# One value unit loaded in two parts: 80 partitions by the GpSimd queue, 48 by the SyncE queue

## The chip, the cores and the metric

The kernel runs on one core of a Trainium2 chip. The metric is the device time of one execution in microseconds (us), as the median of several runs. Kernels that are compared ran on the same chip in alternation. The spans in the profile are shorter than the times by about 2 us.

Words used below: a *DMA engine* is one of the sixteen that move bytes for this core. *SP* is SyncE, whose queue issues nearly all loads; *POOL* is GpSimd. A *share* is one partition's row of 16 KB; it moves as one packet (the trace of the kernel before has 9216 packets of 16,384 bytes for its 72 loads of 128 such rows). A *completion* is one of the sixteen increments of a load's semaphore that DMA makes (the traces record sixteen for each of these loads); that each of the sixteen engines makes one when its part has landed is how the author reads them.

## The reference, cut to what matters

One token goes through two branches, whose results are mixed by a gate. The heavy branch is attention over a long cache.

```
q = (x @ wq)                              # 32 heads of 128; x is [1, 1, 1024]
k_cache, v_cache: [1, 4, 65536, 128] bf16 # 64 MB each: read once
scores = q k^T * 128**-0.5; p = softmax(scores); o = p v
a = o @ wo
b = mixer(x, w_in, w_sp, b_sp, w_out)     # 7 + 4 MB of weights
out = g * a + (1 - g) * b                 # g = sigmoid(sum(x * gate_w))
```

All in all 162 MB come from HBM for very little arithmetic.

## The kernel before

The caches are read in units of 8192 keys, 2 MB each. A unit is `[128 partitions, 8192]` in bf16: partition p holds 64 keys that follow one another, so a partition's row is 16 KB in one piece. Loads go into a ring of nine slots, in one order, all from the SP queue. A slot is loaded again as soon as TensorE has read it.

```python
def kv(cache, g, u):
    return cache[0, g, UK * u:UK * (u + 1), :].rearrange("(p x) d -> p (x d)", p=128)
...
def issue(upto):
    while issued[0] < min(upto, len(stream)):
        n = issued[0]
        assert n < NS or stream[n - NS][0] in used
        key, src, ln = stream[n]
        s = n % NS
        P("SP", lambda e, n=n, src=src, ln=ln: e.dma_start(slot(n)[:, 0:ln], src), w=[("slot", s)], dma="s%d" % s)
        issued[0] += 1
...
# the order: wq (4 loads); then K units, with w_in and w_out between them;
# from the ninth K unit on a K and a V unit in turn; then V units; then wo (4 loads)
...
def pv_piece(n):                      # one V unit: 16 matmuls
    sl, key = use(("v", n))
    ...
    P("PE", f, r=[("ptsb", n % 2), key], w=[B(OB)])
    issue(place[("v", n)] + NS + 1)
```

Of the kernel before, what the change touches and what calls it, by code (L numbers as in the profile page):

```python
# [8 lines left out]
ALU = mybir.AluOpType  # L9
# [7 lines left out]
class Recorder:  # L17
# [7 lines left out]
        self.readers = {}  # L25
        self.dma_count = {}

    def op(self, eng, fn, r=(), w=(), dma=None):
        o = Op()
        o.eng, o.fn, o.inc, o.count = eng, fn, False, 0  # L30
        o.dma = None
        deps = {}
        for k in r:
            if k in self.writer:
                deps[id(self.writer[k])] = (self.writer[k], True)
        for k in w:
            if k in self.writer:
                deps.setdefault(id(self.writer[k]), (self.writer[k], False))
            for x in self.readers.get(k, ()):
                deps.setdefault(id(x), (x, False))  # L40
        o.deps = list(deps.values())
        for k in r:
            self.readers.setdefault(k, []).append(o)
        for k in w:
            self.writer[k] = o
            self.readers[k] = []
        if dma is not None:
            self.dma_count[dma] = self.dma_count.get(dma, 0) + 16
            o.dma = (dma, self.dma_count[dma])
        o.idx = len(self.ops)  # L50
        self.ops.append(o)
        return o
# [85 lines left out]
def bass_gated_mix__gqa_block_cached__mixer_gmlp__decode_kernel(  # L138
# [23 lines left out]
    FC = FH // 128  # L162
# [3 lines left out]
    NU = Sk // UK  # L166
# [5 lines left out]
    QW = DO // 4  # L172
# [9 lines left out]
    def region(name, nbf):  # L182
        nonlocal cur
        OFF[name] = cur
        cur += (nbf + 31) // 32 * 32

    for name, n in [
        ("RING", NS * SLOT), ("KT", NKTS * 1024), ("SC", NSC * 1024), ("PSB", 1024), ("PTSB", 1024),
        ("QPAD", G * 128), ("IDB", 128), ("IDF", 256), ("BM", 256), ("ONES", 256), ("SEL", 16 * 32),
        ("M16", 32), ("M8", 16), ("M32", 64), ("MQ", 32), ("OT", 256), ("XT", KC), ("GW", KC), ("WB", 2), ("MAXC", 2 * G * NU), ("LP", 2 * G * NU),  # L190
        ("COLS", 2 * 64), ("DM", 32), ("OSB", 1024), ("OSC", 512), ("OV", OC), ("Z", 2 * 28), ("Z2", 2 * 28),
        ("ZG", 2 * 28), ("ZE", 2 * 28), ("YB", FC), ("BROW", 2 * QW), ("OROW", QW),
    ]:
        region(name, n)
    NA = (cur + 63) // 64 * 64
# [2 lines left out]
    def ab(name, n, o=0):  # L198
        return arena[:, OFF[name] + o:OFF[name] + o + n]
# [4 lines left out]
    def vw(base, off, dims, p0=0, np_=128):  # L204
        ps = base.ap[0][0]
        return bass.AP(tensor=base.tensor, offset=base.offset + off + p0 * ps,
                       ap=[[ps, np_]] + [list(d) for d in dims])
# [19 lines left out]
    def slot(n):  # L227
        return ab("RING", SLOT, (n % NS) * SLOT)
# [4 lines left out]
    ptsb = lambda i: ab("PTSB", 512, 512 * (i % 2))  # L233
# [3 lines left out]
    SCB, PTB, OB, MB = 4, 5, 6, 7  # L237
# [4 lines left out]
    P = R.op  # L242

    def B(i):
        return ("bank", i)
# [35 lines left out]
    WQ_N = HQ * Dh  # L281
# [20 lines left out]
    for n in range(NU, total + NU + 1):  # L302
        k = n if n < total else None
        v = n - NU - 1
# [4 lines left out]
        else:  # L309
            v = None  # L310
# [3 lines left out]

    issued = [0]

    def issue(upto):
        while issued[0] < min(upto, len(stream)):
            n = issued[0]
            assert n < NS or stream[n - NS][0] in used  # L320
            key, src, ln = stream[n]
            s = n % NS
            P("SP", lambda e, n=n, src=src, ln=ln: e.dma_start(slot(n)[:, 0:ln], src), w=[("slot", s)], dma="s%d" % s)
            issued[0] += 1

    used = set()
# [1 line left out]
    def use(key):  # L328
        issue(place[key] + 1)
        used.add(key)  # L330
        return slot(place[key]), ("slot", place[key] % NS)

    issue(NS)


    P("DVE", lambda e: e.tensor_reduce(m8, vw(idf, 0, [[1, 8], [8, 16]]), AXX, ALU.add), r=["idf"], w=["m8"])
# [5 lines left out]
      r=["m32"], w=["sel"])  # L342
# [6 lines left out]
      r=["ones", "gs"], w=[B(PTB)])  # L349
# [4 lines left out]
      r=["g"], w=["omg"])  # L354


    for i in range(4):
        sl, key = use(("wq", i))

        def f(e, i=i, sl=sl):  # L360
            for k in range(2):
                for h in range(HQ):
                    ins = e.matmul(pf(OB)[:, h:h + 1], sl[:, WQ_N * k + 128 * h:WQ_N * k + 128 * (h + 1)],  # L363
                                   xT[:, 2 * i + k:2 * i + k + 1], start=(i == 0 and k == 0 and h == 0),
                                   stop=(i == 3 and k == 1), skip_group_check=True)
            return ins
        P("PE", f, r=["xT", key], w=[B(OB)])
        issue(place[("wq", i)] + NS + 1)
    for g in range(G):
        P("DVE", lambda e, g=g: e.tensor_copy(vw(qpad, 128 * g, [[40, 4], [1, 8]]),  # L370
                                              vw(pf(OB), 8 * g, [[0, 4], [1, 8]])),
          r=[B(OB)], w=["qpad"])
# [75 lines left out]
    def pv_piece(n):  # L448
        g, u = KV[n]
        sl, key = use(("v", n))  # L450

        def f(e):
            for xi in range(4):
                for cg in range(4):
                    ins = e.matmul(pf(OB)[32 * cg:32 * (cg + 1), :],  # L455
                                   ptsb(n)[:, 128 * xi + 32 * cg:128 * xi + 32 * (cg + 1)],
                                   vw(sl, 128 * (4 * cg + xi), [[2048, 4], [1, 128]]),
                                   start=(u == 0 and xi == 0), stop=(u == NU - 1 and xi == 3),
                                   tile_position=(0, 32 * cg), skip_group_check=True)
            return ins  # L460
        P("PE", f, r=[("ptsb", n % 2), key], w=[B(OB)])
        issue(place[("v", n)] + NS + 1)
        if u == NU - 1:
            out_piece(g)
# [104 lines left out]
    for si, (k, v, aux) in enumerate(steps):  # L569
        nxt = steps[si + 1][1] if si + 1 < len(steps) else None  # L570
        if k is None and pend:
            s_piece()
        if v is not None and v not in started:
            start_exp(v)
        for j in range(4):
            if k is not None:
                k_piece(k, j)
                s_piece() if len(pend) > 1 else None
            if j == 1 and v is not None:
                pt_piece(v)  # L580
            if j == 2 and nxt is not None and (k is not None or not pend):
                start_exp(nxt)
            if j == 3 and v is not None:
                pv_piece(v)
        if v is not None and v % NU == 0:
            weight_piece(v // NU)
        if aux is not None:
            (win_piece if aux[0] == "win" else wout_piece)(aux[1])
# [3 lines left out]
    for i in range(4):  # L592
        sl, key = use(("wo", i))
# [11 lines left out]
      r=["brow"], w=["orow", B(FB)])  # L605
# [32 lines left out]
```

## Time and profile before

| | before |
|---|---|
| time, median of the first three runs | 395.02 us (394.99 to 395.49) |
| span in the profile | 393.2 us |
| DMA, slices 3 to 38 | 419 to 430 GB/s |
| TensorE busy | 70% |
| the last load's sixteen completions | 381.95 to 388.62 us |

These are lines of the profile page of the kernel before: the span; the busy tenths and the rate of DMA in 40 equal slices; the DMA queues with packets, megabytes and their share of sixteen engines' span (q1 is the SP queue, q8 carries instructions); the chain of waits by engine and by line; and issues of loads, with the median time from issue to landing.

```profile
span 393.2 us, 8544 instructions
DMA  8999999999999999999999999999999999999992
GB/s 318 403 427 422 419 429 423 423 423 428 430 427 427 424 425 425 427 427 426 423 423 425 427 428 428 427 428 428 427 425 427 421 428 425 427 426 430 425 397 89
q1 hardware_dynamic: 11240, 162.01, 97.3%
q8 instruction: 31, 0.51, 0.5%
DMA 60%; PE 31%; DVE 6%; ACT 1%; issue 1%; ACTq 0%; DVEq 0%
...
arena<-in_A_v_cache_dram SPq DMA_DIRECT2D x32, 2048.0 KB, 37.5
```

The rate is flat from the third slice to the end. Nothing but more rate, or fewer bytes, or a shorter tail can make this kernel faster. The next lines are the end of the chain of waits, in order of time (start, duration, what):

```profile
346.71 41.91 DMA arena<-in_A_wo_dram
388.62 0.14 issue
388.76 1.91 PE pb L598 x26
390.69 0.42 DVE arena L604
```

The last completion of the last load, at 388.62 us, releases the last 1.9 us of matmuls. What counts is therefore the slowest DMA engine's last completion. The semaphore records in the trace give the sixteen completions of a load. Three of them, sorted (us):

```
landing near  40: 39.59 39.65 39.68 39.69 39.78 39.79 39.80 39.82 39.84 39.87 39.88 39.90 39.91 39.92 40.01 40.21
landing near 245: 240.07 240.15 240.19 240.21 240.22 240.64 240.77 242.13 243.34 243.39 243.44 244.89 244.93 244.97 244.99 245.18
the last load:    381.95 382.07 382.08 382.10 382.56 382.72 382.85 385.01 386.78 386.87 388.27 388.33 388.34 388.38 388.40 388.62
```

The engines drift apart, from 0.6 to 6.7 us. The drift grows in steps of about 1.4 us, one engine at a time, and each step falls on one of q8's 16 KB instruction packets (while 30 of these ran, between 46 and 373 us, the sixteen completions' lateness against the median of their first four, summed, grew from 2.9 to 52.1 us). At the end eight engines are late, and the other eight have nothing to do for up to 6.7 us. This is what the change aims at.

### The profile page before, as it was taken

The numbers are of one execution on the slowest core, as the hardware profiler recorded it, in microseconds if no ns is written. First come the engines' busy times: TensorE is split into PE (matmuls) and PEld (weight loads), VectorE is DVE, ScalarE is ACT, GpSimd is POOL, SyncE is SP. The second block draws the span as 40 slices with busy tenths as digits, with TensorE's granted clock in tenths as the row PEclk, the third lists the DMA queues.
The fourth block names the chain that finished last, engine by engine and source line by source line (L and its number), as shares of the span: only waits on it lengthen the run. The fifth ranks groups of instructions, "written<-read, shape, count | busy, mean of one in ns | idle before, by whom it ended". The sixth has DMA issues, their size and how long they took to land.

```text
span 393.2 us, 8544 instructions
## 1 busy us (share of the span) xinstructions
PE 275.8 (70%) x3902; PEld 195.3 (50%) x3902; DVE 160.4 (41%) x347; ACT 124.3 (32%) x171; POOL 1.5 (0%) x8
## 2 busy tenths in 40 slices
PE   0000699996998999997867686779668875644543
PEld 0000688885776766665645464556445553211121
DVE  2000043446666766576534354466334454200200
ACT  1000033332556555553524242335233334210000
POOL 1000000000000000000000000000000000000000
PEclk9999999886999999998989698889888898555555
DMA  8999999999999999999999999999999999999992
GB/s 318 403 427 422 419 429 423 423 423 428 430 427 427 424 425 425 427 427 426 423 423 425 427 428 428 427 428 428 427 425 427 421 428 425 427 426 430 425 397 89
DMA packets 12620, 162.57 MB, mean 413 GB/s; under 512 B 2596, under 2 KB 2600, under 8 KB 2600
## 3 DMA queue, kind: packets, MB, share of 16 engines
q1 hardware_dynamic: 11240, 162.01, 97.3%
q8 instruction: 31, 0.51, 0.5%
q10 hardware_dynamic: 1344, 0.00, 0.2%
q14 instruction: 5, 0.04, 0.0%
HBM read 162.01 MB, written 0.00 MB: 412 GB/s over the span
## 4 chain that ended last, share of the span: by engine, by line
DMA 60%; PE 31%; DVE 6%; ACT 1%; issue 1%; ACTq 0%; DVEq 0%
DMA arena<-in_A_k_cache_dram 30%; PE pb L388 16%; DMA arena<-in_A_wo_dram 11%; DMA arena<-in_gate_w_dram 10%; DMA arena<-in_A_v_cache_dram 10%; PE pb L410 6%; DVE arena L396 3%; PE pb L503 3%; PE pb L455 2%; PE pb L363 2%; DVE arena L415 2%; PE pb L443 1%; ACT arena L393 0%; PE pb L598 0%; PE pb L551 0%
## 5 line engine op out<-in xcount | busy, mean ns | idle before, releaser
L388 PE MATMUL pb<-arena 128*128 128x128 bf16 x2048 | 154.4, 236 | 27.5 <-DMA arena<-in_A_k_cache_dram 27.5
L388 PEld LDWEIGHTS pb<-arena 128*128 128x128 bf16 x2048 | 133.1, 107 | 55.6 <-DMA arena<-in_A_k_cache_dram 33.1
L396 DVE COPY arena<-pb 128x1024 bf16<-128x1024 bf16 x160 | 108.4, 689 | 109.8 <-PE pb L388 109.0
L393 ACT ACTIVATE arena<-pb 128x1024 bf16<-128x1024 bf16 x96 | 97.9, 1020 | 161.8 <-PE pb L388 161.8
L410 PE MATMUL pb<-arena 128*32 128x512 bf16 x512 | 54.9, 419 | 5.5 <-DVE arena L415 3.6
L455 PE MATMUL pb<-arena 128*32 128x512 bf16 x512 | 40.1, 441 | 19.0 <-DMA arena<-in_A_v_cache_dram 18.3
L455 PEld LDWEIGHTS pb<-arena 128*32 128x32 bf16 x512 | 14.3, 104 | 32.8 <-issue 20.2
L348 PE MATMUL pb<-arena 128*128 128x1 f32 x2 | 0.6, 362 | 40.7 <-DVE arena L347 40.7
L436 ACT ACTIVATE arena<-arena 128x512 bf16<-128x512 f32 x32 | 22.8, 713 | 16.3 <-PE pb L443 14.5
L446 DVE COPY arena<-pb 128x512 bf16<-128x512 bf16 x32 | 13.6, 424 | 30.4 <-PE pb L443 30.4
L410 PEld LDWEIGHTS pb<-arena 128*32 128x32 bf16 x512 | 13.3, 93 | 22.0 <-DVE arena L415 6.6
L415 DVE TENSOR_SCALAR_CACHE_REDUCE arena<-pb 128x512 f32<-128x512 f32 x32 | 21.8, 681 | 2.8 <-PE pb L410 2.8
L348 PEld LDWEIGHTS pb<-arena 128*128 128x128 f32 x2 | 0.5, 310 | 40.7 <-DVE arena L347 40.7
L443 PE MATMUL pb<-arena 128*128 128x128 bf16 x128 | 15.4, 257 | 0.0
L346 DVE TENSOR_TENSOR arena<-arena 128x8 f32<-128x8 bf16 x1 | 0.2, 166 | 37.0 <-DMA arena<-in_gate_w_dram 37.0
L443 PEld LDWEIGHTS pb<-arena 128*128 128x128 bf16 x128 | 9.1, 113 | 11.7 <-issue 11.7
L598 PE MATMUL pb<-arena 128*1 128x256 bf16 x128 | 7.5, 413 | 8.8 <-DMA arena<-in_A_wo_dram 8.8
L503 PEld LDWEIGHTS pb<-arena 128*128 128x128 bf16 x224 | 12.3, 153 | 0.9 <-issue 0.9
L503 PE MATMUL pb<-arena 128*128 128x1 bf16 x224 | 12.6, 192 | 0.0
L350 ACT ACTIVATE arena<-pb 128x1 f32<-128x1 f32 x1 | 0.2, 171 | 34.2 <-PE pb L348 34.2
L598 PEld LDWEIGHTS pb<-arena 128*1 128x1 bf16 x128 | 3.7, 115 | 12.3 <-DMA arena<-in_A_wo_dram 6.7
L363 PE MATMUL pb<-arena 128*128 128x1 bf16 x256 | 7.1, 165 | 1.8 <-issue 1.8
(78 smaller groups left out, 60.5 us busy)
## 6 DMA issues: line engine op xcount, KB each, us to landing
arena<-in_A_k_cache_dram SPq DMA_DIRECT2D x32, 2048.0 KB, 29.9
arena<-in_A_v_cache_dram SPq DMA_DIRECT2D x32, 2048.0 KB, 37.5
arena<-in_A_wq_dram SPq DMA_DIRECT2D x4, 2048.0 KB, 14.8
arena<-in_A_wo_dram SPq DMA_DIRECT2D x4, 2048.0 KB, 41.9
arena<-in_B_w_in_dram SPq DMA_DIRECT2D x4, 1792.0 KB, 22.5
arena<-in_B_w_out_dram SPq DMA_DIRECT2D x2, 1792.0 KB, 15.1
arena<-in_A_x_dram ACTq DMA_DIRECT2D x1, 2.0 KB, 22.3
arena<-in_gate_w_dram ACTq DMA_DIRECT2D x1, 2.0 KB, 39.0
```

The costliest lines, as they stand in the source:

```text
L363: ins = e.matmul(pf(OB)[:, h:h + 1], sl[:, WQ_N * k + 128 * h:WQ_N * k + 128 * (h + 1)], xT[:, 2 * i + k:2 * i + k + 1], start=(i == 0 and ...
L388: ins = e.transpose(pbf(pb)[:, 128 * t:128 * (t + 1)], sl[:, 128 * (8 * b + t):128 * (8 * b + t + 1)], idb)
L393: P("ACT", lambda e, i=i, pb=pb: e.activation(ktb(i), pbf(pb), ACTF.Copy), w=[("kt", i % NKTS), B(pb)])
L396: P("DVE", lambda e, i=i, pb=pb: e.tensor_copy(ktb(i), pbf(pb)), w=[("kt", i % NKTS), B(pb)])
L410: ins = e.matmul(pf(SCB)[32 * cg:32 * (cg + 1), :], qpad[:, 128 * g + 32 * j:128 * g + 32 * (j + 1)], src, start=(j == 0), stop=(j == 3), ...
L415: P("DVE", lambda e: e.tensor_scalar(scs(n), pf(SCB), 0.0, None, op0=ALU.add, op1=ALU.max, accum_out=maxc[:, n:n + 1]), w=[("sc", n % NSC) ...
L436: P("ACT", lambda e: e.activation(psb(n), scs(n), ACTF.Exp, bias=gcol(g, K_NB), scale=SCALE, accum_out=lp[:, n:n + 1]), r=[("sc", n % NSC) ...
L443: ins = e.transpose(pbf(PTB)[:, 128 * xi:128 * (xi + 1)], psb(n)[:, 128 * xi:128 * (xi + 1)], idb)
L446: P("DVE", lambda e: e.tensor_copy(ptsb(n), pbf(PTB)[:, 0:512]), w=[("ptsb", n % 2), B(PTB)])
L455: ins = e.matmul(pf(OB)[32 * cg:32 * (cg + 1), :], ptsb(n)[:, 128 * xi + 32 * cg:128 * xi + 32 * (cg + 1)], vw(sl, 128 * (4 * cg + xi), [[ ...
L503: ins = e.matmul(pf(MB)[:, z:z + 1], vw(sl, c0, [[7, 128]]), xT[:, 2 * i + k:2 * i + k + 1], start=(i == 0 and k == 0 and z == 0), stop=(i ...
L598: ins = e.matmul(pf(FB)[32 * q:32 * q + 1, 0:QW], ovec[:, 8 * i + c:8 * i + c + 1], sl[:, DO * c + QW * q:DO * c + QW * (q + 1)], start=(i ...
```

## The change

The intent is to give the early engines more of one unit and the late engines less. In the unit of group 2 with u = 0 (unit 16 of 32), partitions 0 to 79 come from the POOL queue in a copy whose source has an outermost dimension of 8, meant to have eight DMA engines carry ten shares each. Partitions 80 to 127 stay with SP, by the author's reckoning on sixteen engines with three shares each. Eight engines would then move 13 shares of this unit and eight move 3, where each moved 8. A tiny copy of 8 x 64 bytes ahead of it, on the same queue, is there to turn the queue's choice of engines. The rest of the diff (a scratch tile, an unused argument) is cut.

```diff
+    BAL = {("v", 2 * NU)}
+    HALF = 80
+    def eights(e, d, s_):
+        n = d.ap[-1][1]
+        m = d.ap[0][1] // 8
+        a = bass.AP(tensor=s_.tensor, offset=s_.offset, ap=[[m * n, 8], [n, m], [1, n]])
+        b = bass.AP(tensor=d.tensor, offset=d.offset, ap=[list(d.ap[0]), [1, 1], [1, n]])
+        return e.add_instruction(mybir.InstDMACopy(..., queue="qPoolDynamic", ins=e.lower_ap_dma(a), outs=e.lower_ap_dma(b)))
     def issue(upto):
 ...
-            P("SP", lambda e, n=n, src=src, ln=ln: e.dma_start(slot(n)[:, 0:ln], src), w=[("slot", s)], dma="s%d" % s)
+            p0 = HALF if key in BAL else 0
+            o = P("SP", lambda e, n=n, src=src, ln=ln, p0=p0: e.dma_start(slot(n)[p0:128, 0:ln], src[p0:128, :]),
+                  w=[("slot", s)], dma="s%d" % s)
+            if p0:
+                o2 = P("POOL", lambda e, n=n, src=src: eights(e, slot(n)[0:HALF, :], src[0:HALF, :]), w=["half"],
+                       dma="half")
+                o2.deps = list(o.deps)
 ...
     issue(NS)
+    P("POOL", ... InstDMACopy(..., ins: A_wq as [[WQ_N, 8], [1, 32]], outs: junk[0:8, :]) ..., dma="junk")
 ...
-        P("PE", f, r=[("ptsb", n % 2), key], w=[B(OB)])
+        P("PE", f, r=[("ptsb", n % 2), key] + (["half"] if ("v", n) in BAL else []), w=[B(OB)])
```

More of the change, by code (lines that the diff above doesn't have):

```diff
@@ L26, in __init__, with op @@
         self.dma_count = {}
-    def op(self, eng, fn, r=(), w=(), dma=None):
+    def op(self, eng, fn, r=(), w=(), dma=None, parts=1):
         o = Op()
@@ L47, in op @@
         if dma is not None:
-            self.dma_count[dma] = self.dma_count.get(dma, 0) + 16
+            self.dma_count[dma] = self.dma_count.get(dma, 0) + 16 * parts
             o.dma = (dma, self.dma_count[dma])
@@ L191, in bass_gated_mix__gqa_block_cached__mixer_gmlp__decode_kernel @@
         ("COLS", 2 * 64), ("DM", 32), ("OSB", 1024), ("OSC", 512), ("OV", OC), ("Z", 2 * 28), ("Z2", 2 * 28),
-        ("ZG", 2 * 28), ("ZE", 2 * 28), ("YB", FC), ("BROW", 2 * QW), ("OROW", QW),
+        ("ZG", 2 * 28), ("ZE", 2 * 28), ("YB", FC), ("BROW", 2 * QW), ("OROW", QW), ("JUNK", 32),
     ]:
@@ L315, in bass_gated_mix__gqa_block_cached__mixer_gmlp__decode_kernel @@
     issued = [0]
+    BAL = {("v", 2 * NU)}
[5 more added lines that the diff above has]
+        b = bass.AP(tensor=d.tensor, offset=d.offset, ap=[list(d.ap[0]), [1, 1], [1, n]])
+        return e.add_instruction(mybir.InstDMACopy(
+            mode="Copy", name=nc.get_next_instruction_name(), engine=e.engine, queue="qPoolDynamic",
+            cce_op=ALU.bypass, ins=e.lower_ap_dma(a), outs=e.lower_ap_dma(b)))
     def issue(upto):
@@ L333, in bass_gated_mix__gqa_block_cached__mixer_gmlp__decode_kernel @@
     issue(NS)
+    junk = ab("JUNK", 32)
+    P("POOL", lambda e: e.add_instruction(mybir.InstDMACopy(
+        mode="Copy", name=nc.get_next_instruction_name(), engine=e.engine, queue="qPoolDynamic", cce_op=ALU.bypass,
+        ins=e.lower_ap_dma(bass.AP(tensor=A_wq.tensor, offset=A_wq.offset, ap=[[WQ_N, 8], [1, 32]])),
+        outs=e.lower_ap_dma(junk[0:8, :]))), w=["junk"], dma="junk")
     P("DVE", lambda e: e.tensor_reduce(m8, vw(idf, 0, [[1, 8], [8, 16]]), AXX, ALU.add), r=["idf"], w=["m8"])
```

## The prediction

> What bounds the kernel. The page's slices show DMA at 9 tenths and some 425 GB/s throughout; q1 fills 97.3% of sixteen engines' span. The chain of waits is 60% DMA; PE is busy 70%. The load queue always holds work (a K load takes 29.9 us from issue to landing, loads land 4.9 us apart), so the time is that of the DMA engine that has most to do, plus 1.9 us of matmuls, 0.4 us of DVE and the output.
>
> Uneven engines. The sixteen completions of each load, lie within 0.65 us at 40 us, 3.5 us at 160 us, 5.1 us at 260 us, and 6.7 us at the last load: seven engines end at 381.95 to 382.85 us, one at 385.01, eight at 386.78 to 388.62. The cause is the packet table's q8: 31 instruction packets of 16 KB, one per 8 to 24 us; the spread grows stepwise, one late engine more by about 1.4 us per packet, going round the same eight engines. The ninth (385.01) is delayed near 181 and 310 us, where q14 packets run.
>
> The change. One V unit: 80 partitions by the GpSimd queue in eight shares of 10, 48 by the SP queue in sixteen shares of 3. [...] Eight engines then move 13 partitions of this unit instead of 8, eight move 3. A 16 KB packet takes 0.613 us, so each group shifts by 5 x 0.613 = 3.1 us. No other engine's instructions change; GpSimd was idle after 2.3 us.
>
> Sum. If the favoured eight are the early eight: late ones end at 388.62 - 3.07 = 385.55, the seven at 385.9, the ninth at 385.01 + 3.07 = 388.1. So the gain is only about 0.5 us; the ninth takes the rest of 2.7. If the eight are the late ones, the end moves to about 391.7 (+3.1 us). [...]
>
> GpSimd's part also overtakes some 30 us of queued loads: for 25 us the favoured engines are 6.1 us later, tiles land up to 3 us later, but the backlog hides it.
>
> Prediction: 394.4 us, range 392.0 to 397.5 (8 in 10). Faster by over 2%: 0.01; within 2%: 0.96; slower: 0.03.
>
> What would show it. Right: the last load's completions lie within about 3 us, one engine last; the GpSimd queue carries 1.3 MB in 80 packets of 16 KB; V unit 16's GpSimd part lands 12 to 15 us after issue, its SP part about 35 us. Wrong: the spread grows to 10 to 13 us (wrong eight); packets over 0.62 us in those stretches[...]; an end below 386.5 us (the ninth was not hit).
>
> [...]

The sum: the last load ends at 388.1 us instead of 388.62, 0.5 us less, which takes the 395.0 us of before to about 394.5; the forecast put 394.4. Its 5 shares rest on the author's reckoning of which engines carry what. Cut is a loss of one to three us that the forecast named as a risk; it was not in the 394.4.

## The result

The changed kernel took 412.23 us in the median of four runs (410.01 to 413.36), and the kernel before, on the same chip, 395.0 us (394.81 to 395.49). The ratio is 1.043 (95% interval 1.038 to 1.048): slower by 4.3%. A ratio here is the mean time of one kernel's runs over that of the other's of the same rounds, so it is not quite the ratio of the medians quoted. The profiled run is the fastest of the four, 410.01 us. What follows explains that run; the three others lost 1.4 to 3.4 us more, and as they have no profile, that part is not explained.

These are the lines of the profile page of the changed kernel that answer to those of before. q0 is the POOL queue.

```profile
span 408.2 us, 8547 instructions
DMA  8999999999999999999999999999999999999991
GB/s 318 416 423 418 425 423 428 421 429 424 424 429 427 420 430 424 427 425 425 429 422 432 360 252 352 416 244 353 424 429 427 421 427 429 430 421 429 432 395 50
q1 hardware_dynamic: 11160, 160.70, 95.9%
q0 software_dynamic: 208, 1.31, 1.3%
q8 instruction: 31, 0.51, 0.5%
DMA 59%; PE 28%; DVE 7%; another core or an unknown queue 3%; ACT 1%; issue 1%; ACTq 0%; DVEq 0%
...
arena<-in_A_v_cache_dram POOLq DMA_DIRECT2D x1, 1280.0 KB, 24.2
arena<-in_A_v_cache_dram SPq DMA_DIRECT2D x1, 768.0 KB, 55.3
```

("Another core or an unknown queue" is a wait that the view could put down to no load; only one core runs.) The engines are as busy as before (the DMA row), but in two places they move less: slices 23 to 25 and slices 27 and 28. The two stretches are where the unit's two parts are moved. POOL's own timeline dates the first: the tiny copy is issued at 2.22 us, the large one at 226.42 us, and it lands 24.2 us later, not 12 to 15. The part of SP lands 55.3 us after its issue, not some 35.

```profile
2.22 0.65 POOL L354 DMA_DIRECT2D arena<-in_A_wq_dram  x1
226.42 0.59 POOL L326 DMA_DIRECT2D arena<-in_A_v_cache_dram  x1 [223.55 <-PE pb L412]
```

The view by stretches gives a number for each. First the kernel before, then the changed kernel; the last two columns are DMA's busy share and GB/s.

```profile
core 0: us, PE busy (x) PEld busy (x) DVE busy (x) ACT busy (x) POOL busy (x), PEclk, DMA share, GB/s
230.00:250.00 20.00, 14.36 (x200) 10.16 (x200) 8.76 (x16) 7.32 (x10) 0.00 (x0) 0.91 1.00 425
262.00:282.00 20.00, 16.13 (x228) 11.57 (x227) 11.10 (x23) 7.72 (x12) 0.00 (x0) 0.93 1.01 428
```

```profile
230.00:250.00 20.00, 8.12 (x100) 5.50 (x100) 4.40 (x8) 3.66 (x5) 0.00 (x0) 0.70 1.00 265
262.00:282.00 20.00, 12.95 (x175) 9.41 (x173) 10.71 (x25) 5.34 (x7) 0.00 (x0) 0.83 1.01 289
```

A loss of rate is a loss of time: 20 x (1 - 265/425) = 7.5 us in the first stretch and 20 x (1 - 289/428) = 6.5 us in the second, 14.0 us in all. The mean of the last load's sixteen completions moved by 13.9 us, from 385.3 to 399.2. The last of them moved by 15.0 us, from 388.62 to 403.63, which is all of what the profiled run lost (395.0 to 410.0):

```profile
361.74 41.89 DMA arena<-in_A_wo_dram
403.63 0.14 issue
403.76 1.91 PE pb L622 x32
405.69 0.43 DVE arena L628
```

So 14 us are lost rate, and the remaining 1.1 us is that the sixteen ended less evenly: their spread grew from 6.7 to 10.7 us, the opposite of the intent. Two of the prediction's three signs of being wrong are thus there at once, that of the wrong eight engines (a spread of 10 to 13 us) and that of packets over 0.62 us (next); only experiments can tell what each cost.

In the packet records the loss shows as longer packets. Between 230 and 250 us the median 16 KB packet took 1.00 us on POOL's queue and 1.02 us on SP's, where it takes 0.613 us before; between 266 and 278 us, where only SP's queue moves data, it took 1.20 us. The number of bytes is the same. DMA did not run out of work either: its busy share stayed at 1.00, so TensorE's longer waits were hidden. In the view of waits between 228 and 285 us, the longest wait for a K load is 3.0 us before and 10.5 us after (columns: total, times, longest):

```profile
PE pb L388 <- DMA arena<-in_A_k_cache_dram: 9.5, 5, 3.0
```

```profile
PE pb L412 <- DMA arena<-in_A_k_cache_dram: 20.1, 4, 10.5
```

### The profile page after: what moved, and what is told of

It reads as the page before. It is cut to its first block, busy times and chain, and to the rows that moved or that the text cites. A ratio compares the mean times of both kernels' runs of the same rounds, so it can differ in the third digit from the quotient of the medians.

```text
span 408.2 us, 8547 instructions
## 1 busy us (share of the span) xinstructions
PE 273.6 (67%) x3902; PEld 193.5 (47%) x3902; DVE 160.2 (39%) x347; ACT 124.5 (30%) x171; POOL 2.6 (1%) x10
## 3 DMA queue, kind: packets, MB, share of 16 engines
q0 software_dynamic: 208, 1.31, 1.3%
## 4 chain that ended last, share of the span: by engine, by line
DMA 59%; PE 28%; DVE 7%; another core or an unknown queue 3%; ACT 1%; issue 1%; ACTq 0%; DVEq 0%
DMA arena<-in_A_v_cache_dram 20%; DMA arena<-in_A_k_cache_dram 20%; PE pb L412 14%; DMA arena<-in_A_wo_dram 10%; DMA arena<-in_gate_w_dram 10%; PE pb L434 5%; DVE arena L420 4%; PE pb L527 3%; PE pb L479 2%; DVE arena L439 2%; PE pb L387 2%; PE pb L467 1%; ACT arena L417 0%; PE pb L622 0%
## 5 line engine op out<-in xcount | busy, mean ns | idle before, releaser
L412 PE MATMUL pb<-arena 128*128 128x128 bf16 x2048 | 152.6, 234 | 41.7 <-DMA arena<-in_A_k_cache_dram 41.7
L412 PEld LDWEIGHTS pb<-arena 128*128 128x128 bf16 x2048 | 131.4, 106 | 70.3 <-DMA arena<-in_A_k_cache_dram 47.5
L467 PE MATMUL pb<-arena 128*128 128x128 bf16 x128 | 15.0, 251 | 0.0
L467 PEld LDWEIGHTS pb<-arena 128*128 128x128 bf16 x128 | 8.8, 111 | 11.1 <-issue 11.1
L527 PEld LDWEIGHTS pb<-arena 128*128 128x128 bf16 x224 | 12.3, 153 | 0.9 <-issue 0.9
## 6 DMA issues: line engine op xcount, KB each, us to landing
arena<-in_A_v_cache_dram POOLq DMA_DIRECT2D x1, 1280.0 KB, 24.2
arena<-in_A_v_cache_dram SPq DMA_DIRECT2D x1, 768.0 KB, 55.3
```

The lines of the kernel that those rows point to most:

```text
L412: ins = e.transpose(pbf(pb)[:, 128 * t:128 * (t + 1)], sl[:, 128 * (8 * b + t):128 * (8 * b + t + 1)], idb)
L467: ins = e.transpose(pbf(PTB)[:, 128 * xi:128 * (xi + 1)], psb(n)[:, 128 * xi:128 * (xi + 1)], idb)
L527: ins = e.matmul(pf(MB)[:, z:z + 1], vw(sl, c0, [[7, 128]]), xT[:, 2 * i + k:2 * i + k + 1], start=(i == 0 and k == 0 and z == 0), stop=(i ...
```

## The experiments

Three theories can explain longer packets. **Place**: engines slow each other down when they write at the same time to certain partitions, and the cut makes them do so. The recorded texts call this theory "ports"; what in the memory would cause it was the author's guess, and no trace shows it, nor the engine of a packet. How many engines a copy of less than 128 partitions takes, and how many shares each gets, is the author's reckoning too. The runs below test only what can be measured: whether time and rate depend on the partitions written. **GpSimd queue**: what POOL issues is slow in itself. **Shape**: unequal shares, or the rows that an engine reads from HBM, are at fault.

### Both parts by SP, and the whole unit by POOL

The first run keeps the cut at partition 80 and takes POOL away. The second keeps POOL and takes the cut away.

```diff
 e1_sp_both
-                o2 = P("POOL", lambda e, n=n, src=src: eights(e, slot(n)[0:HALF, :], src[0:HALF, :]), w=["half"],
+                o2 = P("SP", lambda e, n=n, src=src, p0=p0: e.dma_start(slot(n)[0:p0, :], src[0:p0, :]), w=["half"],
                        dma="half")
-    (the tiny copy)

 e2_pool_all
+            if key in BAL:
+                P("POOL", lambda e, n=n, src=src, ln=ln: e.dma_start(slot(n)[:, 0:ln], src), w=[("slot", s)],
+                  dma="half")
-    (both parts, the tiny copy)
```

> The same cut of the unit into partitions 0 to 79 and 80 to 127, but both parts by the SP queue[...]; no GpSimd copy at all. Theory 'ports'[...]: packets of over 0.9 us in one stretch of 10 to 25 us, and 402 to 410 us. Rival 'GpSimd queue'[...]: packets stay at 0.61 us, and 394 to 396 us. Rival 'uneven work' (eight engines have 13 shares): 394 to 396 us, since all engines get 5 + 3 = 8.

> The whole unit of 128 partitions by the GpSimd queue in one ordinary copy[...]. Ports: packets stay near 0.61 us[...], 394 to 396 us. GpSimd queue: packets at one microsecond and the rate down to about 60%, 399 us or more.

Both parts by SP: 406.1 us (405.3 to 406.8) against 395.5, ratio 1.027 (1.025 to 1.028). The whole unit by POOL: 395.24 us against the same 395.5, ratio 0.999 (0.998 to 1.001). The stretch in which e1's two parts were moved:

```profile
252.00:274.00 22.00, 15.47 (x174) 11.01 (x174) 11.21 (x26) 7.32 (x10) 0.00 (x0) 0.76 1.01 240
```

So the GpSimd queue costs nothing here: its 128 packets had a median of 0.615 us. Nor, it seems, are unequal amounts needed: in e1, by the author's reckoning, every engine has 5 + 3 = 8 shares, as before (no trace shows it; the DMA share in the stretch is 1.01), and it still loses 10.6 us. The GpSimd theory falls. What is left is the cut.

### The same unit in three pieces

In e3 partitions 32 to 95 go by SP, and the rest, 0 to 31 and 96 to 127, by two POOL copies of the form that had at most eight packets in flight in the changed kernel. e4 adds tiny copies around them. The author assumed that e3's pieces keep out of each other's way or do not, depending on which engines POOL's first copy gets, and that the tiny copies swap the engines of the two; neither had been shown.

```diff
 e3_quarters
+                o = P("SP", lambda e, n=n, src=src: e.dma_start(slot(n)[32:96, :], src[32:96, :]), ...)
+                for a, b, h in ((0, 32, "half"), (96, 128, "half2")):
+                    o2 = P("POOL", lambda e, n=n, src=src, a=a, b=b: eights(e, slot(n)[a:b, :], src[a:b, :]), w=[h], dma=h)
-    (the two parts of 80 and 48, the tiny copy)

 e4_quarters_shifted: the same, and
+    cursor(0)     # a copy of 8 x 64 bytes ahead, as in the changed kernel
 ...
+    cursor(1)     # and one behind
```

> The unit as partitions 32 to 95 by the SP queue[...], and 0 to 31 and 96 to 127 by two GpSimd copies on eight engines each[...]. [...] Ports: one of this run and the next stays at 394 to 396 us with packets of 0.61 us, the other has packets of over 0.9 us and takes 398 to 406 us. GpSimd queue or uneven work: both runs alike.

> As the run before, but one copy of 8 x 64 bytes[...] goes ahead on the GpSimd queue and one behind[...]. Ports: the opposite of the run before (one at 394 to 396 us, one at 398 to 406 us). GpSimd queue or uneven work: the same as the run before within 1 us.

Neither was slow: 395.42 us and 394.99 us against 395.48 us, ratios 1.000 and 0.999, packets with a median of 0.61 us. Cutting a unit in three, with half of it on POOL, costs nothing here. But one of the two was expected to be slow. Either the tiny copies did not turn the engines round, or the place does not matter. The pair did not tell these apart, so the question was put again with both orders in one execution.

### Both orders in one kernel

Units 16 and 24 are both cut as in e3. In unit 16 POOL first issues partitions 0 to 31, in unit 24 first 96 to 127.

```diff
 e8_both_orders (against e3_quarters)
-    BAL = {("v", 2 * NU)}
+    BAL = {("v", 2 * NU), ("v", 3 * NU)}
-                for a, b, h in ((0, 32, "half"), (96, 128, "half2")):
+                cut = [(0, 32, "half"), (96, 128, "half2")]
+                for a, b, h in (cut if key[1] == 2 * NU else cut[::-1]):
```

> V units 16 and 24 each as SP 32 to 95 and two GpSimd copies of 32 partitions on eight engines; unit 16 has the copy of 0 to 31 first, unit 24 that of 96 to 127 first. [...] Ports[...]: one unit runs at 0.61 us a packet, the other shows packets of about 1.2 us for 5 to 10 us, and the time is 397 to 400 us. If [...]ports do not matter: both units at 0.61 us, 394 to 396 us.

It took 400.61 us (400.1 to 401.06), just above the expected range, against 395.07, ratio 1.013 (1.011 to 1.015). The two units, by stretches:

```profile
228.00:243.00 15.00, 8.60 (x135) 5.69 (x133) 5.00 (x9) 5.70 (x9) 1.21 (x2) 0.91 1.02 429
300.00:315.00 15.00, 6.73 (x100) 4.55 (x100) 4.30 (x8) 3.66 (x5) 0.00 (x0) 0.90 1.01 278
```

The second stretch in e3_quarters, where unit 24 is an ordinary load:

```profile
300.00:315.00 15.00, 12.66 (x171) 9.39 (x172) 8.01 (x15) 5.28 (x7) 0.00 (x0) 0.89 1.02 429
```

Unit 16 runs at the full 429 GB/s, unit 24 at 278 GB/s with a median packet of 1.03 us. Pieces, bytes and queues are the same in both; only the order of the two copies is exchanged. That fits the place theory if the order decides which engines write which 32 partitions; that it does is the author's reading, as no trace shows the engine of a packet. No run has the same order in both units, so this run alone does not exclude that a second pair of POOL copies is slow for being the second; the next runs do without POOL.

### The same reads to other partitions

To separate reading from writing, SP moves one half of a unit. In e5 the unit is cut at 64, with a right result. In e6 and e7 only rows 0 to 63 of four V units are loaded (the result is wrong), in e6 to partitions 0 to 63, in e7 to 32 to 95.

```diff
 e5_halves
+                o = P("SP", lambda e, n=n, src=src: e.dma_start(slot(n)[0:64, :], src[0:64, :]), ...)
+                o2 = P("SP", lambda e, n=n, src=src: e.dma_start(slot(n)[64:128, :], src[64:128, :]), ...)

 e6_low64, e7_mid64: BAL = {("v", 2 * NU + i) for i in range(4)}, and
-                P("SP", lambda e, n=n, src=src: e.dma_start(slot(n)[0:64, :], src[0:64, :]), ...)     # e6
+                P("SP", lambda e, n=n, src=src: e.dma_start(slot(n)[32:96, :], src[0:64, :]), ...)    # e7
```

> The unit by the SP queue in two copies, partitions 0 to 63 and 64 to 127[...]; right result. [...] Ports: packets of about 1.2 us for some 10 us, 399 to 402 us. Rival 'shape' (shares that are not whole groups of four rows, or engines with unequal shares, are slow for another reason, such as the reads from HBM): here every engine has four rows that follow one another, so 394 to 396 us.

> Wrong result on purpose: of four V units only rows 0 to 63 are loaded, to partitions 0 to 63, by the SP queue. 4 MB less in all, worth 4 x 2.45 = 9.8 us. Ports: [...]nothing or little is saved: 392 to 397 us, packets of about 1.2 us. Reads from HBM or shape: 384 to 387 us, and the same as the next run.

> Wrong result on purpose: as the run before, with the same rows read[...], but written to partitions 32 to 95[...]. Ports: 384 to 387 us and packets of 0.61 us, some 10 us less than the run before. Reads from HBM or shape: as the run before, within 1 us.

The halves took 404.75 us, ratio 1.024 (1.022 to 1.026), with this line for their stretch:

```profile
252.00:274.00 22.00, 15.08 (x174) 10.77 (x170) 11.11 (x26) 7.33 (x10) 0.00 (x0) 0.74 1.00 242
```

Four half units to partitions 0 to 63 took 410.28 us, ratio 1.039; the same bytes from the same rows to partitions 32 to 95 took 385.36 us, ratio 0.975, with the kernel before at 395.07 us. First e6, then e7, in the same stretch:

```profile
255.00:309.00 54.00, 31.30 (x383) 22.27 (x381) 19.27 (x40) 13.83 (x20) 0.00 (x0) 0.75 1.01 228
```

```profile
255.00:309.00 54.00, 43.33 (x639) 29.97 (x636) 29.55 (x60) 24.11 (x35) 0.00 (x0) 0.97 1.01 427
```

Between e6 and e7 only the destination partitions differ, and the time differs by 24.9 us. Reads from HBM and the shape of the shares are out; this settles that it is the place of writing. The 228 GB/s of e6 is close to what eight engines working alone would move, an estimate: 8 x 16,384 bytes in 0.613 us are 214 GB/s. Two expectations missed in size, both on the low side: e5 was to take 399 to 402 us and took 404.75, and e6, for which the author guessed that little or nothing would be saved, was to come out at 392 to 397 us, and it took 410. That is some 15 us more. Between 252 and 309 us the median packet took 1.19 us (0.613 in e7). Three quarters took over 1.04 us, and two thirds of them all belong to K units, which were loaded in the ordinary way, so these were slowed too. Why the slowness spreads so far was not tested.

### Which eight engines

The last question about the change is whether it also picked the wrong engines. Here the tiny copy gets a second counting dimension (16 rows as 8 x 2) and stands behind the large copy or ahead of it. The author assumed that a tiny copy of this form turns the queue's choice of engines and that the changed kernel's, counted in one dimension, does not, so that in e10 the late engines would get the ten shares; no trace had shown it.

```diff
 e9_turn_behind, e10_turn_before
-            ins=e.lower_ap_dma(bass.AP(..., ap=[[WQ_N, 8], [1, 32]])), outs=e.lower_ap_dma(junk[0:8, :])
+            ins=e.lower_ap_dma(bass.AP(..., ap=[[2 * WQ_N, 8], [WQ_N, 2], [1, 32]])),
+            outs=e.lower_ap_dma(bass.AP(..., ap=[list(d.ap[0]), [1, 1], [1, 32]]))      # d = junk[0:16, :]
 e9: after the whole program; e10: ahead, where the changed kernel has it
```

> The changed kernel, but its tiny copy comes behind the large GpSimd copy and is shaped with a second counting dimension (16 rows as 8 x 2)[...]. If so, [...]the time is 409 to 412 us, within 1.5 us from run to run. If the tiny copy plays no part: 410 to 413.4 us, scattered as the changed kernel is.

> As the run before, with the tiny copy ahead of the large one[...]. Ports: packets slow in the same two stretches; the late engines get more to do as well, so the last load's landings lie 10 us or more apart, with the late group last, and 411 to 418 us. If the wrong eight engines, and not the ports, were what cost the changed kernel its time, this run would be at 395 us or less.

Behind: 412.57 us (409.86 to 413.24), ratio 1.043, the same as the changed kernel; its scatter is the same too (3.4 us, where under 1.5 was expected), so the alternation that I suspected behind that scatter is not supported. Ahead: 417.25 us (416.69 to 419.06), ratio 1.058. The last load's completions, first, last and mean (us):

```
changed kernel   392.92  403.63  mean 399.2
e9_turn_behind   392.64  403.32  mean 399.1
e10_turn_before  396.27  410.32  mean 403.0
```

With the two-dimensional tiny copy ahead the kernel takes 4.7 us more than with it behind (417.25 against 412.57 us). The one-dimensional tiny copy makes no difference: with it ahead (changed kernel, 412.23 us) or with none ahead (e9, 412.57 us) the large copy behaves alike. That the first turns the choice of engines and the second does not is the author's reading; how many engines a tiny copy uses, and which, no trace shows. Neither order comes near 395 us: on that reading the wrong eight engines are not what cost most of the time.

### The balance by layout instead

If handing a unit's partitions to other engines makes writing slow, bytes can be moved to other partitions. The 1024 rows of a weight that is contracted with x need not lie eight to a partition. Nine rows on partitions 0 to 63 and seven on 64 to 127 should relieve the engines that write the upper half; that an engine keeps to its partitions was assumed (e12's first line below bears on it). e11 does this to the mixer's first weight (rows of 7 KB), e12 to wq (rows of 8 KB). TensorE gets 28 or 32 more matmuls with 64 rows each.

```diff
 e12_wq_by_port (against the kernel before; e11 alike for w_in)
+    small(xw[0:64, :], A_x from 897 on, every second element, "xw")
 ...
+                parts = [slot[:, 0:WQ_N] <- A_wq rows 768 + 2p, p in 0..127]
+                parts += [slot[b:b+32, WQ_N:2*WQ_N] <- rows 769 + 2(b + p) for b in (0, 32)]  # SP, 8 x 4 rows
+                wqc[b:b+32, :] <- rows 897 + 2(b + p) for b in (0, 32)                    # the ninth row
 ...
-            for k in range(2):
+            for k in range(3 if i == 3 else 2):
+                np_ = 64 if i == 3 and k else 128
```

> The kernel before with the balance made by the layout: of the 1024 rows of the mixer's first weight, partitions 0 to 63 hold nine each and 64 to 127 seven each, instead of eight each; the extra rows come by the SP queue in copies of 32 partitions[...]. No GpSimd copy. Ports, with the late engines those of partitions 64 to 127: late engines do 7168 x 8 bytes less, 2.15 us; they end at 386.5 instead of 388.6, the delayed early one at 387.2, and the time is 1.0 to 1.6 us below the kernel before. If the late engines were those of partitions 0 to 63: 2 us above it. If no engine can be relieved: no difference.

> The balance by layout again, moved to the query weight, where every ring slot stays full: in the run before (the mixer weight) the ring ran dry near 110 us, as a slot with half a load in it made the buffer shallower. Partitions 0 to 63 hold nine rows of 8 KB, 64 to 127 seven; the ninth row goes to a buffer that is unused until the first scores. Late engines do 8192 x 8 bytes less, 2.45 us, and end at 386.2; the delayed early engine ends at 385.0 + 2.45 = 387.5. Ports and layout: 393.7 to 394.7 us, 0.5 to 1.2 us below the kernel before. If the ring runs dry here as well, or the 32 added matmuls at the start delay the rest: 395.5 us or more. The last load's landings lie within 5 us.

Neither beat the kernel before: e11 took 396.87 us against 395.04 (ratio 1.004, 1.003 to 1.005), e12 397.29 us against 395.2 (1.005, 1.004 to 1.007). In e11 the ring also ran dry for some microseconds near 110 us: its rate fell to 375 GB/s in slice 12. e12 had no such gap, and is the cleaner answer. Its completions (us):

```
landing near  31: 25.79 25.87 25.89 25.92 26.00 26.07 26.12 26.28 | 30.89 30.91 30.95 31.03 31.04 31.05 31.12 31.23
the last load:    379.81 380.23 384.33 384.73 384.88 384.93 385.37 385.66 385.90 385.91 386.10 386.16 386.17 387.65 389.48 390.82
```

At 31 us the two halves of the engines stand 5 us apart, as two rows of eight partitions should make it (2 x 8 x 8 KB at 26.7 GB/s are 4.9 us). So layout does move work between engines, at full rate (424 GB/s in slices 3 and 4, where the kernel before has 427 and 422). But at the end two engines of the lower half are last, at 389.48 and 390.82: those are late *and* got more. 388.4, where late engines end in the kernel before, plus the added 2.45 us is 390.8. And two engines end at 379.8 and 380.2, as relieved ones would that were never late (382.1 to 382.8 less 2.45). The late eight are thus not one half of the engines; read this way they are six of the upper half and two of the lower. That is worked out from the times, not seen.

The completions of the other runs can test this reading. Take the sixteen of the kernel before, move all by the mean shift of a run, then move eight of them up and the other eight down, by 3.07 us for a cut unit and by 2.45 us for e12, and try every choice of eight. The sorted result comes closest to the run's own completions when the eight are five early engines, the delayed one and two late ones, in e12 (root mean square difference 0.12 us), in the changed kernel (0.54) and in e9 (0.55); in e10 it does with the other eight, two early and six late (0.59). The prediction's picture, seven early and the delayed one, leaves 1.76 us in the changed kernel, and all late ones leave 2.00 us in e10. The delayed one is the least certain: without it the changed kernel still fits to 0.60 us. So the halves are mixed in all four runs. The completions do not carry the engines' numbers, so which engines of a half are late stays open, and a layout that fits them was not tried.

## Why the prediction was wrong

**What bounds the kernel, and the drift: right.** The span is the slowest engine's last completion plus 4.6 us, in both kernels (393.2 - 388.6 and 408.2 - 403.6); in the changed kernel too, the whole loss of the profiled run (15.0 us) is the shift of that completion. The drift grew as the prediction says; that instruction packets cause it rests on steps and packets falling together in time.

**Eight engines with ten shares, sixteen with three: it fits.** q0 shows 1.31 MB, 80 packets of 16 KB among them. Which engines carried them is not seen, but at most eight of the 80 are in flight at once, and the completions fit two groups of eight that are moved apart by 2 x 3.07 us.

**"Each group shifts by 5 x 0.613 = 3.1 us": the step that failed.** It took a share's time from ordinary loads (0.613 us), and let the cost stay with the engine that has the share. While the unit's two parts were moved, the median packet took 1.02 and 1.20 us, those of other loads included. A sum of +3.1 us for eight engines and -3.1 for eight has a mean of zero; the measured mean was +13.9 us. As a difference between the two groups the 3.1 us fits; that it is all that the cut does to the engines is what failed.

**A loss of one to three us from the place of writing: the right risk, mis-sized and thought unlikely.** The term measured 7.5 + 6.5 = 14.0 us. There was no working for the one to three. What the runs show is that the slowness does not stay with the unit's own shares: the rate of all sixteen engines falls to 265 and 289 GB/s for as long as the parts are moved. What slows the loads beside them is not seen. The argument against the risk was that packets are long for another reason too: q8's took 1.08 us in the kernel before, and the 30 data packets over 0.9 us that overlap one took 1.10 (medians). That says nothing of a second reason beside it.

**"If the favoured eight are the early eight": wrong as a picture.** I read seven early, one delayed and eight late engines as two halves. e12's two last engines point to two late ones among the lower eight, and the completions of the changed kernel fit two late engines among the favoured (the last two, at 403.48 and 403.63 us; the next is at 401.73). So, as an estimate, even with no cost of the place the end would have come at 386.78 + 3.07 = 389.9 us or later, at least 1.2 us after that of before, where the prediction had a gain of 0.5. The 1.1 us that the lost rate leaves over is of this size.

**The tiny copy: wrong.** It was to turn the queue's choice of engines, an assumption. It changed no time (412.23 us in the changed kernel, 412.57 in e9; 394.99 in e4, 395.42 in e3).

**"The backlog hides it": right** for what it spoke of. TensorE waited up to 10.5 us, and DMA stayed busy throughout.

## What to carry to other kernels

When DMA is at its limit, ask of every load not only how many bytes it moves but which partitions it writes. Here loads of 128 partitions (425 to 429 GB/s), or of 32 to 95 (427 in e7), ran at full rate; loads of 0 to 63 (228 in e6), of both halves (242 in e5), or of 80 and 48 partitions (240 in e1, 265 and 289 in the changed kernel) did not, the loads beside them included. The cause behind this is not shown. To move work between engines, move bytes between partitions (e12: two groups 5 us apart at full rate). First learn which engines are late: a sorted list of completion times shows how many, not which, until a known shift is put on one half of them.
